# An attention and MLP kernel on one core: MLP tiles placed between the head pairs

## The chip, the cores and the metric

The kernel runs on one core of a Trainium2 chip. The metric is the device time of one execution in microseconds, as the median of several runs. A profiled execution has its own time, and its span is the time from its first to its last recorded instruction.

## The reference

```python
# q, k, v: (8, 8, 576, 64), s: (8, 8, 576); w_ch1: (512, 2048), w_ch2: (2048, 512); all float32
scores = matmul(q, k.T) / 8
cum = cumsum(maximum(s, 0))
scores = where(causal, -1e9, scores + minimum(-(cum[:, None] - cum[None, :]), 0))
scores = scores - max(scores)
attn = exp(scores);  attn = attn / (sum(attn) + 1e-9)
x = (attn @ v), heads side by side: (8, 576, 512)
u = x + real(fft(fft(x, axis=1), axis=2))
un = (u - mean(u)) / sqrt(var(u) + 1e-6)
out = u + maximum(un @ w_ch1, 0) @ w_ch2
```

## The kernel before

**Attention** goes over 32 head pairs, `i = 0..31`, four to a batch. `load` brings q and k, `high` and `low` split them into a high part and a rest (so that a product is made of two matmuls), `maxes(i)` makes 12 score matmuls (`pm`) of which DVE keeps each row's maximum, and a transpose (`pmt`) brings the maxima into a row of the q operand. `scores(i)` makes the scores again, transposed and with maximum and bias inside (`ps`, 24 matmuls), and ACT turns them into `P` with an exponential. `av(i)` multiplies by v (`pavA`, `pavB`), `recip` and `finish` divide by the row sums. In pair `i` the pieces of several pairs run together: scores of `i`, AV of `i - 1`, maxima of `i + 1`, splitting of `i + 2`.

**Fourier.** After the last pair of a batch, `folds` uses the symmetry of the transforms (DVE, ACT, POOL), and `fourier` makes two passes of matmuls (`pzs`, `pzc`, `pyc`, `pys`) and writes `u` to DRAM (`uD`). One more product for frequency 256 (`p256`) is made once for four batches. Batch `b` is folded in pair `4b + 6` and mixed in pairs `4b + 7` to `4b + 10`.

**MLP.** The 4608 tokens make nine tiles of 512. `ln_tile` reads a tile of `u`, makes means and variances with matmuls against a matrix of `1/512`, and leaves the centred values in two parts, `uch` and `ucl`, in one of two sets of buffers that tiles use in turn. For each of 16 slices `f` of the hidden width, `mlp_tile` makes twelve matmuls into a bank `h`, ACT writes `zh` (relu), DVE the rest `zl`, and twelve matmuls add to four banks `acc`. These 24 matmuls are called a block here; there are 144. The weights come as int64 words (`wP`) from which `rounded` makes float32 values in a few integer steps on DVE, ACT and POOL. `convert_w` does so for the first six slices during attention and stores them in `wD`; `load_w` takes them, or converts the other ten itself while the first MLP tile runs, and splits them into `wh` and `wl`, which then stay in SBUF.

**Order.** `weave` takes generators with a total cost each and always lets the one advance that has done the smallest share of its total. So the Python code writes instructions in an interleaved order. For TensorE this order is kept through the loop over pairs and its tail (`manual_schedule`); the other engines, and TensorE after `order.close()`, are ordered by the scheduler, which starts from it. Every engine executes its own list in order. Nearly all DMAs are issued by SP.

**PSUM** has eight banks: `ps` gives three (scores, Fourier, `h`), `psm` five (maxima, transposes, AV). For the MLP, `psm` is closed and four of its banks become `acc`.

Of the kernel before, what the change touches and what calls it, by code (L numbers as in the profile page):

```python
# [19 lines left out]
S = 576  # L20
# [7 lines left out]
NC = 6  # L28
NC1 = 4.5
N0 = 3  # L30
N1 = 8
# [10 lines left out]
def fused_kernel(ctx, tc, qkT, vA, sP, wP, tabD, tabS, corr, out):  # L42
# [7 lines left out]
    ps = ctx.enter_context(tc.tile_pool(name="ps", bufs=3, space=PSUM))  # L50
# [4 lines left out]
    wD = dram.tile([NF, 128, 1024], F32, name="wD")  # L55
# [10 lines left out]


# [4 lines left out]
    WC = 256  # L72

    def rounded(pool, f, x, bufs):

        m = pool.tile([128, WC], I32, tag="wm", name="wm", bufs=bufs)
        raw = pool.tile([128, 2 * WC], I32, tag="raw", name="raw", bufs=bufs)
        nc.sync.dma_start(out=raw, in_=wP[f, :, WC * x:WC * x + WC].bitcast(I32))
        hi = raw.rearrange("p (n w) -> p n w", w=2)[:, :, 1]
        lo = raw.bitcast(U16).rearrange("p (n w) -> p n w", w=4)[:, :, 1]  # L80
        yield 0.0
        e = pool.tile([128, WC], I32, tag="we", name="we", bufs=bufs)
# [3 lines left out]
        yield 0.4  # L86
# [3 lines left out]
        yield 0.4  # L90
        return e.bitcast(F32)

    def convert_w(pool, lo, hi, bufs):

        for f in range(lo, hi):
            for x in range(1024 // WC):
                m = yield from rounded(pool, f, x, bufs)
                nc.sync.dma_start(out=wD[f, :, WC * x:WC * x + WC], in_=m)
                yield 0.2

    def load_w(pool, f):

        wh = pool.tile([128, 1024], F32R, tag=f"wh{f}", name=f"wh{f}")
        wl = pool.tile([128, 1024], F32R, tag=f"wl{f}", name=f"wl{f}")
        W[f] = (wh, wl)
        if f < NC:
            nc.sync.dma_start(out=wl.bitcast(F32), in_=wD[f])
        n = 512 if f < NC else WC
        for x in range(1024 // n):
            xs = slice(n * x, n * x + n)  # L110
            m = wl[:, xs].bitcast(F32) if f < NC else (yield from rounded(stage, f, x, nstage))
            nc.scalar.copy(wh[:, xs], m)  # L112
            yield 0.2 * n / 512
            (nc.vector if x * n < 512 else nc.gpsimd).tensor_sub(wl[:, xs], m, wh[:, xs].bitcast(F32))  # L114
            yield 0.2 * n / 512

    def spread_sum(t, name, n):

        th = lnp.tile([128, TOK], F32R, tag="th", name="th")
        tl = lnp.tile([128, TOK], F32R, tag="tl", name="tl")  # L120
        split(th[:, :n], tl[:, :n], t[:, :n])
        m = bank(name)
# [4 lines left out]
    def ln_tile(t0, n, lag):  # L127

        u = lnp.tile([128, 4, TOK], F32, tag="u", name="u")
        (nc.sync if t0 else nc.scalar).dma_start(out=u[:, :, :n], in_=uD[:, :, t0:t0 + n].rearrange("c p t -> p c t"))  # L130
        t = lnp.tile([128, TOK], F32, tag="t", name="t")
        t2 = lnp.tile([128, TOK], F32, tag="t2", name="t2")
        nc.gpsimd.tensor_add(t[:, :n], u[:, 0, :n], u[:, 1, :n])
        nc.vector.tensor_add(t2[:, :n], u[:, 2, :n], u[:, 3, :n])
        nc.vector.tensor_add(t[:, :n], t[:, :n], t2[:, :n])
        yield lag
        pm = spread_sum(t, "mu", n)
        mlp = mlps[t0 // TOK % 2]
# [22 lines left out]

    LN, W = {}, {}

    def mlp_tile(t0, n):
        uch, ucl, mu, r = LN.pop(t0)
        last = t0 + n == NT
        if last:
# [645 lines left out]
```

## Time and profile before

| | |
|---|---|
| median of three runs | 1426.8 us (1423.96 to 1429.57) |
| profiled execution | 1426.1 us, span 1424.4 us |
| mean granted TensorE clock | 0.971 |
| busy share of the span | PE 92%, weight loads 75%, DVE 52%, POOL 39%, ACT 38% |
| DMA | 125.05 MB moved, HBM read 76.85 MB and written 23.07 MB |

PE is TensorE's matmuls, PEld its loads of weights, which overlap them. DVE, ACT and POOL are the vector, scalar and general engines. A matmul is drawn from its start to its modelled end, so two that follow each other closely overlap in the drawing, and the busy share of PE says little on how full it is. In rows of groups, `zh<-h` is what an instruction writes and reads, `x144` how often it ran, then busy time, mean ns of one, and the engine's idle time before it with what ended it.

### The profile page before, as it was taken

The numbers are of one execution on the slowest core, as the hardware profiler recorded it, in microseconds if no ns is written. First come the engines' busy times: TensorE is split into PE (matmuls) and PEld (weight loads), VectorE is DVE, ScalarE is ACT, GpSimd is POOL, SyncE is SP. The second block draws the span as 40 slices with busy tenths as digits, with TensorE's granted clock in tenths as the row PEclk, the third lists the DMA queues.
The fourth block names the chain that finished last, engine by engine and source line by source line (L and its number), as shares of the span: only waits on it lengthen the run. The fifth ranks groups of instructions, "written<-read, shape, count | busy, mean of one in ns | idle before, by whom it ended". The sixth has DMA issues, their size and how long they took to land.

```text
span 1424.4 us, 17997 instructions
## 1 busy us (share of the span) xinstructions
PE 1305.1 (92%) x6190; PEld 1068.7 (75%) x6190; DVE 745.7 (52%) x1684; ACT 539.3 (38%) x1211; POOL 561.6 (39%) x543
## 2 busy tenths in 40 slices
PE   4887979897988887997899999999999999999998
PEld 3766868686777676775688888888888888888886
DVE  6667677877777788799833233222332223322212
ACT  4775756676665656344321121211212112121110
POOL 6445465656546566565720402204022040123300
PEclk9998999999999997999899999999999999999999
DMA  8555556565655555433200000000000000000000
GB/s 214 156 159 144 163 149 180 158 168 159 159 161 144 166 149 163 162 123 121 79 8 30 31 30 15 15 30 31 30 15 15 30 30 30 15 16 0 30 0 30
DMA packets 78230, 125.05 MB, mean 88 GB/s; under 512 B 11256, under 2 KB 36249, under 8 KB 78139
## 3 DMA queue, kind: packets, MB, share of 16 engines
q1 hardware_dynamic: 75627, 119.83, 28.4%
q0 software_dynamic: 1696, 2.50, 0.9%
q10 hardware_dynamic: 816, 1.57, 0.3%
q8 instruction: 49, 0.80, 0.2%
q14 instruction: 42, 0.34, 0.1%
HBM read 76.85 MB, written 23.07 MB: 70 GB/s over the span
## 4 chain that ended last, share of the span: by engine, by line
PE 51%; DVE 7%; POOL 2%; DMA 1%; issue 1%; ACT 1%; SPq 0%; DVEq 0%; POOLq 0%; ACTq 0%
PE h L183 25%; PE acc L198 8%; PE acc L196 8%; PE acc L197 8%; POOL we L89 1%; DVE wm L88 1%; DVE we L83 1%; DVE wm L85 1%; DVE we L87 1%; DVE wl L114 1%; ACT wh L112 1%; DMA wl<-wD 0%; POOL wl L114 0%; DVE ucl L148 0%; DVE zl L188 0%
## 5 line engine op out<-in xcount | busy, mean ns | idle before, releaser
L188 DVE SCALAR_TENSOR_TENSOR zl<-h,zh 128x512 fp32r<-128x512 f32 x144 | 98.6, 686 | 405.5 <-ACT zh L187 405.4
L187 ACT ACTIVATE zh<-h 128x512 fp32r<-128x512 f32 x144 | 85.9, 596 | 530.1 <-PE h L183 530.1
L198 PE MATMUL acc<-zl,wh 128*128 128x512 f32 x576 | 227.5, 396 | 4.9 <-DVE zl L188 4.9
L196 PE MATMUL acc<-zh,wh 128*128 128x512 f32 x576 | 227.6, 395 | 1.0 <-ACT zh L187 1.0
L197 PE MATMUL acc<-zh,wl 128*128 128x512 f32 x576 | 226.8, 394 | 0.0
L523 PE MATMUL pavB<-P,va 128*128 128x320 f32 (+2 forms) x640 | 189.1, 389 | 9.5 <-ACT stage L527 8.9
L459 PE MATMUL pm<-KQ 128*128 128x256 f32 (+3 forms) x384 | 156.5, 427 | 44.4 <-DVE Mx L466 23.1
L495 ACT ACTIVATE P<-ps 128x320 f32<-128x320 f32 (+4 forms) x384 | 145.9, 393 | 110.5 <-PE ps L492 106.8
L491 PE MATMUL ps<-KQ 128*128 128x256 f32 (+2 forms) x384 | 154.1, 404 | 24.4 <-ACT P L495 14.0
L183 PE MATMUL h<-uch,wh 128*128 128x512 f32 x576 | 159.9, 398 | 8.3 <-ACT wh L112 8.3
L183 PE MATMUL h<-uch,wl 128*128 128x512 f32 x576 | 158.1, 396 | 0.8 <-DVE wl L114 0.8
L183 PE MATMUL h<-ucl,wh 128*128 128x512 f32 x576 | 156.9, 393 | 0.0
L466 DVE CUSTOM_DVE_ANT_0 trash<-pm,amask 128x128 bf16<-128x128 f32 (+3 forms) x256 | 123.5, 482 | 34.2 <-PE pm L459 16.9
L212 POOL TENSOR_TENSOR o<-o,w 128x512 f32<-128x512 f32 x32 | 41.8, 1305 | 252.3 <-issue 218.5
L183 PEld LDWEIGHTS h<-uch,wh 128*128 128x128 f32 x576 | 108.2, 190 | 35.9 <-ACT wh L112 12.1
L198 PEld LDWEIGHTS acc<-zl,wh 128*128 128x128 f32 x576 | 108.7, 189 | 32.0 <-DVE zl L188 6.9
L183 PEld LDWEIGHTS h<-uch,wl 128*128 128x128 f32 x576 | 109.2, 190 | 26.6 <-DVE wl L114 1.2
L196 PEld LDWEIGHTS acc<-zh,wh 128*128 128x128 f32 x576 | 108.6, 188 | 26.1 <-ACT zh L187 1.8
L183 PEld LDWEIGHTS h<-ucl,wh 128*128 128x128 f32 x576 | 108.9, 189 | 24.7
L197 PEld LDWEIGHTS acc<-zh,wl 128*128 128x128 f32 x576 | 108.6, 189 | 24.7
L459 PEld LDWEIGHTS pm<-KQ 128*128 128x128 f32 x384 | 78.4, 207 | 64.7 <-DVE Mx L466 30.2
L492 PE MATMUL ps<-q,k 128*128 128x256 f32 (+2 forms) x384 | 120.5, 316 | 3.1 <-POOL q L438 3.1
(140 smaller groups left out, 2066.9 us busy)
## 6 DMA issues: line engine op xcount, KB each, us to landing
qk<-in_qkT_dram SPq DMA_DIRECT2D x32, 576.0 KB
raw<-in_wP_dram SPq DMA_DIRECT2D x64, 256.0 KB
va<-in_vA_dram SPq DMA_DIRECT2D x32, 480.0 KB
q<-KQ SPq DMA_DIRECT2D x32, 288.0 KB
k<-KQ SPq DMA_DIRECT2D x32, 288.0 KB
rb<-rd SPq DMA_DIRECT2D x64, 144.0 KB
u<-uD SPq DMA_DIRECT2D x8, 1024.0 KB
out_dram<-o SPq DMA_DIRECT2D x32, 256.0 KB
```

The lines of the kernel that those rows point to most:

```text
L183: nc.tensor.matmul(h[:, :n], a[:, j * 128:(j + 1) * 128], b[:, j, :n], start=i == 0, stop=i == 11)
L187: nc.scalar.activation(zh[:, :n], h[:, :n], AF.Relu)
L188: nc.vector.scalar_tensor_tensor(out=zl[:, :n], in0=h[:, :n], scalar=0.0, in1=zh[:, :n].bitcast(F32), op0=ALU.max, op1=ALU.subtract)
L196: nc.tensor.matmul(acc[j][:, :n], a[:, cs], y[:, :n], start=g == 0, stop=False)
L197: nc.tensor.matmul(acc[j][:, :n], b[:, cs], y[:, :n], start=False, stop=False)
L198: nc.tensor.matmul(acc[j][:, :n], a[:, cs], z[:, :n], start=False, stop=g == NF - 1)
L459: nc.tensor.matmul(p[:, :n], qy[:, h, 128 * c:128 * c + 128], ky[:, h, k0:k0 + n], start=True, stop=True)
L466: nc.vector.tensor_tensor_reduce(out=trash[:nq, :n], in0=p[:nq, :n], in1=amask[:nq, m0:m0 + n], scale=1.0, scalar=first if x else NEG, op0 ...
L491: nc.tensor.matmul(p[:, :n], ky[:, h, ksl], qy[:, h, a:a + n], start=True, stop=False)
L492: nc.tensor.matmul(p[:, :n], k1[:, h, ksl], q1[:, h, a:a + n], start=False, stop=True)
L495: nc.scalar.activation(P[:, o:o + a + n - lo], p[:, lo - a:n], AF.Exp, scale=0.125)
L523: nc.tensor.matmul(p[:, a - lo:n], va[:, c, vs], P[:, o:o + w], start=c == 0, stop=c == cs[-1])
```

## The change

- From the tenth pair on (`M0 = 9`), each weave also holds four blocks of the MLP (`RATE = 4`), 2.5 in five more weaves after the last pair; what is left runs at the end. The generator `mlp()` runs through all 144 blocks in one go, with the layer norm of the next tile at `f` = 8, 10 and 12 or 15. It waits, by yielding, until the batch that the next tile needs is in `ready`.
- All sixteen slices of weights are converted in pairs 0 to 12, ten of them (`NC = 10`) in pairs 0 to 8, in pieces of 512 columns that use the buffers `uch` and `ucl`, the others in pieces of 256. They are split there, and both parts go to `wD`. Each block then fetches its weights, 0.5 MB for `h` and 0.5 MB for `acc`, into two buffers each (`fetch`). After the last pair, slices are kept as they are fetched: seven in room that attention leaves (`NA = 7`), nine more when Fourier is done.
- PSUM: `ps` and `psm` have four banks each until pair 9. From there `psm` is `acc`, and scores, maxima, transposes, AV, Fourier and `h` share the four of `ps`.
- Buffers: three `P` in place of four, two `qk` in place of three, one `rb`, one `xs`; Fourier and folds share their scratch. Until Fourier is done there is one set of `uch` and `ucl`. `u` is read from DRAM a quarter at a time, three times a tile, into three buffers `uj` that also hold the parts for the sums and the output.
- `p256` is made for each batch, with the frequency's column among 128 others; Fourier is mixed in two pairs (`4b + 7`, `4b + 8`), not four.

```diff
-NC = 6
-NC1 = 4.5
-N0 = 3
-N1 = 8
+NC = 10
+NA = 7
+M0 = 9
+RATE = 4
...
-    ps = ctx.enter_context(tc.tile_pool(name="ps", bufs=3, space=PSUM))
+    ps = ctx.enter_context(tc.tile_pool(name="ps", bufs=4, space=PSUM))
...
+    def convert(f, x, wc, words, m, e):
+        k, o = divmod(x * wc, 512)
+        nc.sync.dma_start(out=words, in_=wP[f, :, wc * x:wc * x + wc].bitcast(I32))
...
+        wh, wl = words[:, 0:wc], words[:, wc:2 * wc]
+        nc.scalar.copy(wh.bitcast(F32R), e.bitcast(F32))
+        (nc.gpsimd if k else nc.vector).tensor_sub(wl.bitcast(F32R), e.bitcast(F32), wh.bitcast(F32))
+        yield 0.3
+        nc.sync.dma_start(out=wD[f, :, k, :, o:o + wc], in_=words.bitcast(F32).rearrange("p (s n) -> p s n", s=2))
...
+    def fetch(k, s):
+        if s >= NS:
+            return
+        f = s % NF
...
+        if f not in W and rooms:
+            W[f] = x = rooms.pop(0).tile([128, 2, 2, 512], F32R, tag=f"W{f}", name=f"W{f}")
+            for h in (k, 1 - k):
+                nc.sync.dma_start(out=x[:, h].bitcast(F32), in_=wD[f, :, h])
+        if f in W:
+            uses[k, s] = W[f][:, k]
+            return
+        w = mlp0.tile([128, 2, 512], F32R, tag=f"w{k}", name=f"w{k}", bufs=2)
+        nc.sync.dma_start(out=w.bitcast(F32), in_=wD[f, :, k])
+        uses[k, s] = w
...
+    def output(x, acc, r):
+        t0, n = tiles[x]
+        for j in range(4):
+            u = uload(x, j)
+            o = mlp0.tile([128, TOK], F32, tag="uj", name="o", bufs=3)
+            nc.vector.tensor_mul(o[:, :n], r[:, :n], acc[j][:, :n])
+            nc.gpsimd.tensor_add(o[:, :n], o[:, :n], u[:, :n])
+            nc.sync.dma_start(out=out[j, :, t0:t0 + n], in_=o[:, :n])
...
+    def mlp():
...
+        for s in range(NS):
+            x, f = divmod(s, NF)
...
+            fetch(0, s + 2)
+            yield C1
+            if x + 1 < len(tiles):
+                early = len(mlps) > 1
+                if f == 8:
+                    while min(x + 1, NB - 1) not in ready:
+                        yield 1.0
+                    lnp[x + 1] = sums(x + 1)
+                if f == 10:
+                    mean(x + 1, *lnp.pop(x + 1))
+                    go = 12 if early else NF - 1
+                if f >= 11 and f == go:
+                    centre(x + 1)
...
+                yield from second(accs[y], held, [(0, j) for j in range(4)], tiles[y][1])
+                del held[0]
+            held.append((uses.pop((1, s)), zh, zl, f))
+            fetch(1, s + 1)
+            if f == 0 and x:
+                output(x - 1, accs.pop(x - 1), rs.pop(x - 1))
...
-    psm = attb_ctx.enter_context(tc.tile_pool(name="psm", bufs=5, space=PSUM))
+    psm = psm_ctx.enter_context(tc.tile_pool(name="psm", bufs=4, space=PSUM))
...
+        if i < M0 + 4:
+            share = NC / (M0 - 0.5) if i < M0 else (NF - NC) / 3.5
+            streams.append([take(weights, share), share + 0.001])
+        if i == M0 - 1:
+            streams.append([later(take(stages, 6), 7), 13])
+        if i == M0:
+            psm_ctx.close()
+            psm = None
+            accp = ctx.enter_context(pool("accp", space=PSUM))
+        if i >= M0:
+            quota = (RATE if i < NP else 2.5) * (C1 + 4 * C2)
+            streams.append([take(stages, quota), quota])
```

How the order changes at two places. TensorE, in a pair in the middle of the loop, before (`pzs` is Fourier, numbers behind a name are buffers):

```order
L523 MATMUL pavA<-P,va 128x256
L459 MATMUL pm<-KQ_121 128x256
L284 MATMUL pzs<-dsin_81,Do_2744 96x256
L284 MATMUL pzs<-dsin_82,Do_2744 96x256
L284 MATMUL pzs<-dsin_81,Do_2745 96x256
L284 MATMUL pzs<-dsin_81,Do_2744 96x256
L284 MATMUL pzs<-dsin_82,Do_2744 96x256
L284 MATMUL pzs<-dsin_81,Do_2745 96x256
L491 MATMUL ps<-KQ_120 128x256
L492 MATMUL ps<-q_2922,k_2923 128x256
L459 MATMUL pm<-KQ_121 128x256
```

and after:

```order
L247 MATMUL h<-uch,w_4769 128x512 x8
L247 MATMUL h<-ucl,w_4769 128x512 x4
L537 MATMUL pm<-KQ_118 128x512
L569 MATMUL ps<-KQ_120 128x448
L570 MATMUL ps<-q_4581,k_4582 128x448
L537 MATMUL pm<-KQ_118 128x256
L537 MATMUL pm<-KQ_118 128x320
L217 MATMUL acc_3949<-zh,w_4804 128x512
L218 MATMUL acc_3949<-zh,w_4804 128x512
L219 MATMUL acc_3949<-zl,w_4804 128x512
L537 MATMUL pm<-KQ_118 128x256
```

Twelve matmuls of `h` and the triples of `acc` now stand between maxima and scores, and `h`, `pm` and `ps` take the same four banks in turn, so that the fifth fill from an `h` on needs a bank that ACT and DVE have emptied.

DVE in a pair near the fourth, before: `we` and `wm` are the converter's, `trash` and `Mx` the maxima's.

```order
L466 ISA Mx_128 128x1
L83 TENSOR_SCALAR we<-raw 128x256
L85 TENSOR_SCALAR wm<-raw 128x256
L88 SCALAR_TENSOR_TENSOR wm<-raw,wm 128x256
L87 SCALAR_TENSOR_TENSOR we<-raw,we 128x256
L466 ISA trash,Mx_128<-pm,amask 128x256
```

and after, where `wide` holds all of the converter's parts:

```order
L89 SCALAR_TENSOR_TENSOR wide<-wide 128x512
L88 SCALAR_TENSOR_TENSOR wide<-wide 128x512
L94 TENSOR_TENSOR wide<-wide 128x512
L84 TENSOR_SCALAR wide<-wide 128x512
L86 TENSOR_SCALAR wide<-wide 128x512
L89 SCALAR_TENSOR_TENSOR wide<-wide 128x512
L88 SCALAR_TENSOR_TENSOR wide<-wide 128x512
L544 ISA trash,Mx_127<-pm,amask 128x256
```

Two pieces of the converter, twice as wide and with the split (L94), stand ahead of a read of maxima where one short piece stood.

More of the change, by code (lines that the diff above doesn't have):

```diff
@@ L224, in fused_kernel @@
     nc.vector.memset(eh.bitcast(F32), 0.0)
[L225 to L227 removed]
     rows = fft.tile([96, S], F32, name="rows")
[L229 to L230 removed]
+    x256 = rows[0:1]
     def load_tables():
@@ L567, in call @@
         fn(*args)
[L569 removed]
+    for i in range(min(2, NP)):
         load(i)
@@ L659, in ahead @@
-    def ahead():
-        while next(feed, None) is not None:
-            yield 1.0
-    op = None
-    feed = rest()
-    for x, (t0, n) in enumerate(tiles):
-        streams = [[mlp_tile(t0, n), NF]]
-        if x == 0:
-            streams.append([chain(idle(1000), mixing), FOURIER * 0.6])
-            streams.append([ahead(), 100])
-        if x + 1 < len(tiles):
-            streams.append([later(ln_tile(*tiles[x + 1], 1), 4 if x else 9), 12])
-        weave(*streams)
+            att_ctx.close()
```

426 lines of the change are left out of this document (206 added, 220 removed).

## The prediction

> **What bounds the kernel now.** I read the page first, then the windows by stage, the chain, the timeline of TensorE inside the attention loop, the waits, and the groups by shape. The windows (us, then busy us of PE, PEld, DVE, ACT and POOL, the granted clock, DMA share, GB/s) cut the run into the loop over head pairs, its tail, the first MLP tile, and the other eight:
>
> ```profile
> 25.60:545.00 519.40, 445.96 (x2490) 376.28 (x2490) 378.32 (x1073) 330.19 (x822) 292.75 (x302) 0.95 0.58 160
> 545.00:572.00 27.00, 20.81 (x102) 17.57 (x101) 23.06 (x41) 17.02 (x37) 17.46 (x14) 0.75 0.52 155
> 572.00:704.60 132.60, 113.49 (x483) 87.53 (x482) 117.44 (x247) 56.13 (x125) 79.88 (x87) 0.95 0.36 124
> 704.60:1424.40 719.80, 714.17 (x3096) 580.72 (x3094) 207.58 (x271) 125.73 (x213) 152.78 (x113) 1.00 0.06 22
> ```
>
> In the last stage TensorE is never free and every other engine is under a third busy. The chain shows its rhythm (start, length): one f step of the MLP, a block here, every 5.56 us, and one tile in 89.8 us (882.51 to 972.28).
>
> ```profile
> 882.51 5.60 PE h L183 x24
> 890.87 2.80 PE h L183 x12
> 896.43 2.80 PE h L183 x12
> ...
> 972.28 5.46 PE h L183 x24
> ```
>
> 144 blocks are 801 us, more than half of the run, and nothing in the change makes a block shorter. What can be won is TensorE's idle time elsewhere. The page's 92% for PE hides it, because the drawn length of a matmul overlaps the next one. The distance from start to start tells more. In a dense piece of the loop:
>
> ```profile
> 312.10 0.28 PE L459 MATMUL pm<-KQ 128*128 128x256 f32 x1
> 312.22 0.31 PE L491 MATMUL ps<-KQ 128*128 128x320 f32 x1
> 312.37 0.31 PE L492 MATMUL ps<-q,k 128*128 128x320 f32 x1
> 312.52 0.28 PE L459 MATMUL pm<-KQ 128*128 128x256 f32 x1
> 312.63 0.70 PE L523 MATMUL pavB<-P,va 128*128 128x320 f32 x2
> 312.93 0.80 PE L306 MATMUL pyc<-scos,zc 96*128 96x290 f32 x3
> 313.57 0.34 PE L459 MATMUL pm<-KQ 128*128 128x384 f32 x1
> 313.75 0.28 PE L491 MATMUL ps<-KQ 128*128 128x256 f32 x1
> 313.87 0.28 PE L492 MATMUL ps<-q,k 128*128 128x256 f32 x1
> 313.99 0.39 PE L459 MATMUL pm<-KQ 128*128 128x512 f32 x1
> 314.22 0.49 PE L523 MATMUL pavB<-P,va 128*128 128x192 f32 x2
> ```
>
> 256 columns take 0.12 us, 320 take 0.15, 384 take 0.18, 512 take 0.23; an AV matmul of 320 is two passes, 0.30. By these, and 0.20 for 448 columns in proportion, a pair's own work is 24 score matmuls 3.4 us, 12 for the maxima 1.8, 14 AV matmuls 3.2 and the transpose: 8.5 us. A batch's Fourier part (75 matmuls of 256 to 290 columns) is about 9.6, so 2.4 a pair. That is 10.9 us. The transposes of the maxima, one a pair, come every 16.2 us ((523.4 - 20.5)/31); the other two rows are the 10th and the 14th:
>
> ```profile
> L471 PE MATMUL pmt<-ident,Mx x32: 270/272/374, 20.5 to 523.4; 128*10 128x128 f32 x32
> 153.22 0.27 PE L471 MATMUL pmt<-ident,Mx 128*10 128x128 f32 x1
> 220.64 0.27 PE L471 MATMUL pmt<-ident,Mx 128*10 128x128 f32 x1
> ```
>
> So TensorE waits some 5.3 us in each pair. The waits that the profile can see are short ones, on maxima and exponentials that have to leave their banks:
>
> ```profile
> PE pm L459 <- DVE Mx L466: 22.4, 11, 5.5
> PE ps L491 <- ACT P L495: 14.0, 17, 2.2
> ```
>
> **The change part by part.** I add four stages, cut at the 10th and the 14th transpose. The profiled execution took 1426.1 us, span 1424.4, and the median is 1426.8, so 1.7 us lies around the span.
>
> *A, to the 10th transpose (153.2 us before).* No MLP yet. Ten of the sixteen weight blocks are converted here instead of about 1.3, each now split into high and low parts as well. The load on DVE in two windows, and, from the groups by shape, the converter's work on it (busy us, mean ns):
>
> ```profile
> 25.60:153.50 127.90, 105.54 (x546) 87.02 (x546) 87.84 (x256) 82.14 (x202) 60.64 (x65) 0.92 0.64 163
> 0.00:25.60 25.60, 10.64 (x25) 6.65 (x26) 19.26 (x54) 10.25 (x15) 18.75 (x30) 1.00 0.68 201
> ```
>
> ```profile
> L83 DVE TENSOR_SCALAR we<-raw 128x256 int32<-128x256 int32 x64 | 29.1, 457 | 1.6 <-DMA raw<-in_wP_dram 1.5
> L85 DVE TENSOR_SCALAR wm<-raw 128x256 int32<-128x256 int32 x64 | 26.0, 406 | 0.0
> L87 DVE SCALAR_TENSOR_TENSOR we<-raw,we 128x256 int32<-128x256 int32 x64 | 31.5, 495 | 0.4 <-ACT we L84 0.2
> L88 DVE SCALAR_TENSOR_TENSOR wm<-raw,wm 128x256 f32<-128x256 uint16 x64 | 31.8, 496 | 1.1
> L114 DVE TENSOR_TENSOR wl<-we,wh 128x256 fp32r<-128x256 f32 x20 | 9.7, 487 | 2.3 <-ACT wh L112 2.2
> ```
>
> The four operations are 1.85 us for 256 columns, 7.4 a block, and half of the split 1.0: 8.4. In pieces of 512 columns some of that is saved; I take 6.9. Then 10.3 x 6.9 - 1.3 x 7.4 = 61 us more. DVE was busy 87.8 + 19.3 = 107 us: 168 of work in what were 153 us. DVE becomes the bound of this stage. The least is 168; at the 0.886 that DVE reaches in the first MLP tile (117.44 of 132.60) it is 190. The converter has only two buffers and each step hops between four engines, so I stay near the upper end: 185, +32. ACT and POOL gain about 3 and 5 us a pair and stay under 0.8.
>
> *B, to the 14th transpose (67.4 us before).* The remaining six blocks of weights are converted in 256-column pieces, and the order shows 4, 4, 1 and 1 MLP blocks in these four intervals: each tile's layer norm waits for a batch that is Fourier-mixed one and a half pairs later. TensorE needs 4 x 8.5 + 10 x 5.56 + 10.8 - 4 = 96 us. For DVE:
>
> ```profile
> 153.50:220.90 67.40, 58.08 (x337) 49.49 (x337) 49.06 (x141) 43.93 (x110) 37.88 (x40) 0.95 0.58 164
> ```
>
> ```profile
> L187 ACT ACTIVATE zh<-h 128x512 fp32r<-128x512 f32 x144 | 85.9, 596 | 530.1 <-PE h L183 530.1
> L188 DVE SCALAR_TENSOR_TENSOR zl<-h,zh 128x512 fp32r<-128x512 f32 x144 | 98.6, 686 | 405.5 <-ACT zh L187 405.4
> ...
> L159 DVE RECIPROCAL r<-r 128x512 f32<-128x512 f32 x9 | 30.1, 3339 | 4.7 <-ACT r L158 4.7
> L148 DVE TENSOR_TENSOR ucl<-u,uch 128x512 fp32r<-128x512 f32 x36 | 27.4, 801 | 6.4 <-ACT uch L147 6.4
> ```
>
> 49 there now, 5.3 weight blocks x 8.4 = 45, less 4 for today's, 10 zl x 0.69 = 7, and about 13 of layer norm (eleven operations at 0.8 and one reciprocal): 110. Between TensorE's 96 and DVE's 110/0.886 = 124 I take the latter, 123: DVE is again the longer one.
>
> *C, the next 18 pairs.* 73 blocks stand in them. TensorE: 18 x 8.5 + 73 x 5.56 + 4 batches x 10.8 + 4 for means and variances = 606 us, 33.7 a pair. DVE has about 12 a pair from the loop (378/32), 2.8 of zl and 4 of layer norm, under 0.6 of it, and ACT under 0.5. What TensorE waits on top is not shown by any row, because eight banks (three and five) become four that scores, maxima, AV, Fourier and h share in one order. Nearest rows: the MLP stage, where 714.17 of 719.80 is busy, gives nothing; the loop gives 5.3 a pair with twice the banks, so up to about 8. In favour of the low end, a fill now has on average 33.7/36 = 0.94 us of other work on either side, and h leaves its bank in 0.60 + 0.69 us. Against it, maxima and scores still stand in runs, and there is a new wait: while attention lives there is only one uch/ucl set, so the next tile is centred after the last h of this one, four times an ACT copy and a DVE subtraction (0.8) behind 3 to 5 us of TensorE work, then the four output products must free acc through three "uj" buffers. I give 2 us a pair to the banks and 5 a tile to that: 3.2 a pair, 58. C is 664 (606 to 750).
>
> *D, the rest.* 61 blocks, 339 us; the last pair's attention and two Fourier batches 32; means and two extra halves of a block 9; 18 for the chain of the last batch (norm, xs, folds) and the acc hand-over of four tiles; 6 from the last matmul to the end, as now: 404 (386 to 425).
>
> Weights by DMA: 1.05 MB a block, 4.2 a pair. At the rate of the MLP stage (22 GB/s at a share of 0.06, 367 GB/s) that is 11.4 us of all sixteen engines; the loop's own 0.58 of 16.2 is 9.4 and u, out and uD about 3.5: 24 of 37 us. It is covered, and fetch(0, s+2) has more than a block of cover; if SP stood behind one load for over 8 us, TensorE would wait for w. The added p256 matmuls cost 1.2 us a batch and are counted.
>
> Sum: 185 + 123 + 664 + 404 = 1376, with 1.7 outside the span 1378 us, 3.4% less than the median.
>
> **The rivals.** *Nearly all idle time goes.* If DVE fills A to its 168, B falls to 106, C waits 12 us in all and D 386: 168 + 106 + 618 + 386 + 2 = 1280. For it speaks the MLP stage, which loses nothing with three banks; against it the runs of short fills.
>
> *Four banks make the woven stage wait more than the loop does (slower).* TensorE's order is fixed, so one late maximum stops MLP matmuls too, which had no such neighbour. For it: the waits above, up to 5.5 us at once, with five banks for maxima alone. At 7 us a pair C is 606 + 126 = 732 and the run 1446. It is slower than 1434 from (58 + 56)/18 = 6.3 us a pair on.
>
> *There is little idle time to fill (no change).* Loads of weights are busy 376.28 of 519.40 in the loop, 0.724, and 580.72 of 719.80, 0.807, where TensorE is saturated. If 0.807 is what full looks like, the loop holds 466 us of work, 131 more than my 335 (32 pairs less what runs after 545 us), of which 92 fall in pairs that get MLP; the waits there are then 1.7 a pair at most and my 58 and 18 shrink by about 45: 1378 + 92 - 45 = 1425. Against it stand the dense rows, where loads follow each other closer than their own length:
>
> ```profile
> 312.11 0.19 PEld L491 LDWEIGHTS ps<-KQ 128*128 128x128 f32 x1
> 312.23 0.19 PEld L492 LDWEIGHTS ps<-q,k 128*128 128x128 f32 x1
> 312.37 0.19 PEld L459 LDWEIGHTS pm<-KQ 128*128 128x128 f32 x1
> ```
>
> A full loop would show 1.0, not 0.807. The Trainium skill, Perfetto Trace Analysis, section Identifying the Most-Contended Engine, says that headroom on TensorE is judged by the busy share of LDWEIGHTS and not of matmuls; by that page's measure this rival is the forecast, and these rows disagree with reading it across stages with matmuls of different widths.
>
> **How the numbers follow.** Forecast (1300 to 1419): 0.60. Nearly all idle time goes: 0.14. No idle time to fill: 0.09. Banks, slower: 0.17. Half a per cent, 7 us, is about what a measurement of this kernel tells from no change, so 1419.7 to 1433.9 is "same": faster 0.74, same 0.09, slower 0.17. The range 1285 to 1450 takes the lower end of the second case and most of the slower one; its ends leave out 0.15.
>
> **What would show it.** The 10th transpose at about 185 us with DVE over 0.85 busy before it, and the 14th at about 308. Between them and the 32nd, a transpose every 37 us, with DVE below 0.65 and the granted clock at 1.0. The last stage has h again every 5.56 us. I am wrong if transposes in the woven stage come over 41 us apart, with waits of h or pm for DVE or ACT (banks) or for w (DMA), or if they come at 34.

## The result: 1567 us, 9.7% slower

The changed kernel takes 1567.3 us (median of four runs, 1557.9 to 1571.1), the kernel before 1427.3 beside it: ratio 1.097, 95% interval 1.092 to 1.103. The forecast was 1378, and its range ended at 1450. The profiled execution has a span of 1568.6 us.

The transposes of the maxima cut it into the forecast's four stages. The group, and the 10th and 14th of it in the timeline (start, length):

```profile
L549 PE MATMUL pmt<-ident,Mx x32: 270/272/415, 20.5 to 1160.3; 128*10 128x128 f32 x32
253.58 0.27 PE L549 MATMUL pmt<-ident,Mx 128*10 128x128 f32 x1
432.09 0.27 PE L549 MATMUL pmt<-ident,Mx 128*10 128x128 f32 x1
```

| stage | forecast | measured |
|---|---|---|
| A, to the 10th transpose | 185 | 253.6 |
| B, to the 14th | 123 | 178.5 |
| C, to the 32nd | 664 | 728.2 |
| D, the rest | 404 | 408.3 |

The windows (us, then busy us of PE, PEld, DVE, ACT, POOL, clock, DMA share, GB/s) about these stages, with C in two pieces, since its first two pairs are not like the others:

```profile
25.00:250.00 225.00, 149.03 (x608) 119.52 (x608) 139.82 (x330) 103.41 (x237) 102.06 (x94) 0.78 0.61 175
250.00:430.00 180.00, 128.36 (x583) 101.28 (x582) 93.15 (x229) 73.83 (x167) 62.02 (x67) 0.85 0.61 182
430.00:545.00 115.00, 78.24 (x341) 61.36 (x340) 56.10 (x130) 39.95 (x91) 40.27 (x38) 0.85 0.62 197
545.00:1160.00 615.00, 592.39 (x2937) 494.37 (x2936) 287.62 (x657) 244.40 (x538) 181.42 (x180) 0.99 0.66 200
1160.00:1568.60 408.60, 389.26 (x1760) 322.22 (x1758) 113.79 (x170) 80.82 (x153) 49.18 (x47) 0.97 0.38 126
```

In the first, DVE is busy 0.62 of the time (139.82 of 225), not 0.886: it is not the bound there, and no engine is. The clock is 0.78. Who waits: SP, whose list also holds every load of q, k and v and the row of maxima (`mt`). Its waits in 25 to 250 us, the longest groups (us in total, times, longest):

```profile
SPq L96 <- POOL wide L94: 45.4, 10, 8.2
SPq L96 <- DVE wide L94: 26.1, 5, 7.8
SPq L552 <- ACT P L573: 18.3, 4, 8.6
SPq L96 <- DVE Mx L544: 16.9, 4, 8.9
SPq L96 <- DMA wide<-in_wP_dram: 10.5, 5, 3.8
```

L96 is the converter's write-back. With two more rows, of 8.5 and 2.9, SP stands there 110 us of 225. In its timeline the rows of cumulative sums for a pair's keys (`cumD`) are issued until 71.85, then nothing for 11 us, and the row sums (`sums`) come behind the write:

```profile
70.82 1.03 SPq L494 DMA_DIRECT2D KQ<-cumD  x1
83.05 0.33 SPq L96 DMA_DIRECT2D wD<-wide  x1
83.91 0.80 SPq L610 DMA_DIRECT2D sums<-stage  x1
```

TensorE's longest waits in 25 to 253:

```profile
PE ps L569 <- DMA KQ<-mt: 23.4, 7, 7.3
PE pm L537 <- DVE Mx L544: 19.8, 15, 3.3
```

From 253 to 546, in B and the first two pairs of C, three waits stand out. The first is for the sums of the first MLP tile, the others are for weights (`w`):

```profile
PE mu L149 <- ACT th L74: 26.4, 1, 26.4
PE h L247 <- DMA w<-wD: 19.8, 1, 19.8
PE acc L217 <- DMA w<-wD: 6.1, 2, 6.0
```

The forecast named such a wait for `w` as a sign of being wrong. In SP's list nothing fetches weights for 21 us; between the two fetches stand the transfers of a pair and those of the converter's last, narrow pieces, of which these are the last two:

```profile
484.20 0.37 SPq L130 DMA_DIRECT2D w<-wD  x1
502.93 0.38 SPq L96 DMA_DIRECT2D wD<-narrow  x1
505.15 0.34 SPq L80 DMA_DIRECT2D narrow<-in_wP_dram  x1
505.55 0.43 SPq L130 DMA_DIRECT2D w<-wD  x1
```

In the woven stage proper, 545 to 1160:

```profile
PE h L247 <- ACT uch L185: 12.0, 4, 3.7
PE pm L537 <- DVE Mx L544: 2.6, 7, 0.9
PE ps L569 <- DVE yp L394: 2.4, 4, 0.6
PE ps L569 <- ACT P L573: 2.2, 5, 1.1
```

Apart from the 12.0 for `uch`, the waits of 0.8 us and more are some 10 us in 615, so four banks cost little that the profile shows. The rival on banks was wrong, although the time came out slower.

### The profile page after: what moved, and what is told of

Its sections match the earlier page's. It is cut to its first block, busy times and chain, and to the rows that moved or that the text cites. A ratio compares the mean times of both kernels' runs of the same rounds, so it can differ in the third digit from the quotient of the medians.

```text
span 1568.6 us, 18552 instructions
## 1 busy us (share of the span) xinstructions
PE 1347.2 (86%) x6244; PEld 1104.4 (70%) x6244; DVE 709.0 (45%) x1562; ACT 550.0 (35%) x1195; POOL 453.7 (29%) x456
## 4 chain that ended last, share of the span: by engine, by line
PE 51%; DMA 6%; issue 4%; DVE 4%; ACT 1%; POOL 1%; SPq 0%; DVEq 0%; POOLq 0%
PE h L247 19%; PE acc L217 6%; PE acc L218 6%; PE acc L219 6%; PE pavB L601 5%; DMA uj<-uD 5%; PE ps L569 2%; PE ps L570 2%; PE pm L537 1%; PE pavA L601 1%; PE pyc L380 1%; PE pys L389 1%; PE pzc L369 1%; PE pzs L361 1%; DVE ucl L186 1%
## 5 line engine op out<-in xcount | busy, mean ns | idle before, releaser
L247 PE MATMUL h<-uch,w 128*128 128x512 f32 x792 | 208.8, 405 | 47.7 <-ACT uch L185 26.3
L247 PEld LDWEIGHTS h<-uch,w 128*128 128x128 f32 x792 | 149.5, 194 | 83.8 <-ACT uch L185 30.7
L601 PEld LDWEIGHTS pavB<-P,va 128*128 128x128 f32 x640 | 128.0, 209 | 55.2 <-issue 10.8
L217 PE MATMUL acc<-zh,w 128*128 128x512 f32 x384 | 156.7, 408 | 6.7 <-DMA w<-wD 6.1
L218 PE MATMUL acc<-zh,w 128*128 128x512 f32 x384 | 152.2, 396 | 0.0
L219 PE MATMUL acc<-zl,w 128*128 128x512 f32 x384 | 152.1, 396 | 0.0
L569 PEld LDWEIGHTS ps<-KQ 128*128 128x128 f32 x384 | 79.3, 206 | 67.6 <-DMA KQ<-mt 25.0
L516 POOL TENSOR_TENSOR q<-qk,q 64x576 fp32r<-64x576 f32 x64 | 95.1, 1504 | 70.4 <-DMA q<-KQ 64.8
L247 PE MATMUL h<-ucl,w 128*128 128x512 f32 x396 | 111.1, 403 | 0.8 <-DVE ucl L186 0.8
L247 PE MATMUL h<-uch,W 128*128 128x512 f32 x360 | 91.8, 398 | 0.0
L247 PEld LDWEIGHTS h<-ucl,w 128*128 128x128 f32 x396 | 77.7, 196 | 18.3 <-DVE ucl L186 1.2
L570 PEld LDWEIGHTS ps<-q,k 128*128 128x128 f32 x384 | 79.3, 206 | 8.6
```

Of the source, the lines that this page charges most:

```text
L217: nc.tensor.matmul(acc[j][:, :n], b[:, 0, cs], y[:, :n], start=g == 0, stop=False)
L218: nc.tensor.matmul(acc[j][:, :n], b[:, 1, cs], y[:, :n], start=False, stop=False)
L219: nc.tensor.matmul(acc[j][:, :n], b[:, 0, cs], z[:, :n], start=False, stop=g == NF - 1)
L247: nc.tensor.matmul(h[:, :n], w[:, a, j * 128:(j + 1) * 128], b[:, j, :n], start=i == 0, stop=i == 11)
L516: nc.gpsimd.tensor_sub(q1[64:128, h], qk[0:64, h], q1[0:64, h].bitcast(F32))
L569: nc.tensor.matmul(p[:, :n], ky[:, h, ksl], qy[:, h, a:a + n], start=True, stop=False)
```

## The experiments

"Without conversion" is e3. Times are of the profiled execution, one run each beside a run of the kernel before, unless an interval is given. DVE's, ACT's, POOL's and SP's lists are ordered by a scheduler; only TensorE's is written by hand, and from the loop over pairs on it is that of the changed kernel in e1 to e10 and e16 (in e6 without the AV matmuls left out). The kernel before, run beside these, has spans of 1419.9 to 1431.4 us, so totals that differ by under some 10 us are not told apart.

| run | span | 10th | to 14th | to 32nd | rest |
|---|---|---|---|---|---|
| before | 1424.4 | 153.2 | 67.4 | 302.8 | 901.0 |
| after | 1568.6 | 253.6 | 178.5 | 728.2 | 408.3 |
| e1 no arithmetic | 1449.6 | 186.8 | 158.0 | 699.6 | 405.3 |
| e2 no transfers | 1495.8 | 235.3 | 151.7 | 699.0 | 409.8 |
| e3 no conversion | 1424.5 | 178.5 | 136.7 | 699.8 | 409.5 |
| e4 write late | 1539.5 | 225.8 | 178.9 | 730.2 | 404.5 |
| e5 no hops | 1492.6 | 246.3 | 142.1 | 698.8 | 405.5 |
| e6 AV thinned | 1415.7 | 167.4 | 134.7 | 707.1 | 406.4 |
| e7 skewed | 1540.8 | 224.2 | 161.4 | 746.4 | 408.7 |
| e8 all before | 1518.8 | 274.7 | 142.8 | 698.0 | 403.3 |
| e9 DVE's part only | 1450.5 | 208.8 | 136.0 | 696.3 | 409.4 |
| e10 ACT's and POOL's only | 1453.4 | 207.6 | 137.8 | 697.8 | 410.2 |
| e11 before, no conversion | 1402.8 | 151.9 | 69.4 | 302.2 | 879.4 |
| e12 gentle | 1533.6 | 214.1 | 98.0 | 663.7 | 557.9 |
| e13 before, small buffers | 1449.7 | 157.3 | 70.2 | 321.2 | 900.9 |
| e14 before, dense | 1520.5 | 224.3 | 105.3 | 299.3 | 891.6 |
| e15 before, both | 1530.7 | 223.6 | 105.8 | 306.9 | 894.4 |
| e16 no conversion, three qk | 1412.0 | 170.2 | 135.6 | 698.0 | 408.2 |
| e17 before, ten blocks at 0.28 a pair | 1489.3 | 172.7 | 76.7 | 343.2 | 896.7 |
| e18 before, dense, write late | 1492.8 | 227.0 | 67.6 | 303.9 | 894.3 |

**The conversion in parts.** In `convert`, e1 leaves out the arithmetic, from its first line to its last, and sends a constant at the write:

```diff
-        nc.vector.tensor_scalar(e, hi, 0x7FF00000, None, op0=ALU.bitwise_and)
...
-        (nc.gpsimd if k else nc.vector).tensor_sub(wl.bitcast(F32R), e.bitcast(F32), wh.bitcast(F32))
```

e2 leaves out the transfers, and e3 both:

```diff
-        nc.sync.dma_start(out=words, in_=wP[f, :, wc * x:wc * x + wc].bitcast(I32))
+        nc.gpsimd.memset(words, 0)
...
-        nc.sync.dma_start(out=wD[f, :, k, :, o:o + wc], in_=words.bitcast(F32).rearrange("p (s n) -> p s n", s=2))
...
-        nc.sync.dma_start(out=w.bitcast(F32), in_=wD[f, :, k])
+        nc.sync.dma_start(out=w.bitcast(F32), in_=wD[0, :, k])
```

> Left out: the converter's arithmetic and split; both transfers stay, and the write-back sends a constant tile, so SP has nothing to wait for at it (the weights are then constants, and the order of TensorE is that of the changed kernel). The changed kernel has its 10th transpose of the maxima at 253.6 us, 178.5 to the 14th, 728 to the 32nd, 408 after it. Theory 1 (SP stands in its list at the write-back until the split is done, and what is queued behind it is late): the stand is gone; 10th transpose at 150 to 170, 100 to 120 to the 14th, total 1390 to 1425. Theory 2 (the bytes of the conversion crowd the DMA engines): nothing changes, 1540 to 1570. Theory 3 (DVE, ACT and POOL are too loaded with the arithmetic): as theory 1. Theory 4 (fewer buffers for P, qk, rb and maxima): 1540 to 1570.

> Left out: both transfers of the converter (the raw words are set to zero by POOL, some 1 us a piece more for POOL; all blocks of the MLP fetch the same first weight block of DRAM, which is written once); the arithmetic stays. Theory 1 (SP stands at the write-back): SP has no write-back, so 10th transpose at 165 to 190, total 1390 to 1430. Theory 2 (bytes): the same. Theory 3 (arithmetic load): still 240 to 255 at the 10th transpose, 1530 to 1570. Theory 4 (fewer buffers): 1530 to 1570.

> Left out: the whole conversion, transfers and arithmetic (all blocks fetch the same first weight block, written once); the order of TensorE stays. What is left over the woven forecast is the cost of the smaller buffers. Theories 1 to 3: 10th transpose at 140 to 155, 95 to 115 to the 14th, total 1370 to 1400. Theory 4 (fewer buffers): 10th transpose still over 220, total over 1520.

Without conversion the span is 144.1 us shorter. With the transfers alone it is 25.1 over that, with the arithmetic alone 71.3, together 144.1: 48 us exist only when both are there, which is when SP has arithmetic to wait for. So theory 1 can hold for a third at most, theory 3, which is the forecast's own in a wider form, holds for half, and the bytes of theory 2 for at most the 25. Theory 4 (smaller buffers), which expected e3 above 1520, fails. None of the three totals lies in a range that was expected of theory 1 or 3. In e2 and e5 the scheduler moved 256-column pieces ahead (DVE had run 62 and 85 of their 108 operations when the tenth set of maxima was read, and e5's 246.3 lies above both of its ranges), so I compare these two by their totals. And e3 shows what no theory had: without any conversion the woven kernel only reaches the time of the kernel before.

**Moving the write-back.** In e4, `back` issues the write of the piece before and `ahead` a read two pieces on:

```diff
+            steps = convert(n // 2, n % 2, 512, words[n], me[:, 0:512], me[:, 512:1024])
+            yield next(steps) / 2
+            back(n - 1)
+            yield next(steps) / 2
+            ahead(n + 2)
```

> All work is done. Only the place and the buffers of the converter's transfers change: the raw words go round four buffers (those of w0 and w1, idle until the MLP starts), each read is issued more than one piece ahead and each write-back a third of a piece after the next has begun; the 256-column pieces keep one buffer, with write and read some steps apart. Theory 1 (SP stands at the write-back): most of the loss goes, 10th transpose at 175 to 195, 120 to 145 to the 14th, total 1400 to 1450. Theory 2 (bytes) and theory 3 (arithmetic load) and theory 4 (fewer buffers): the same bytes, work and buffers, 1540 to 1570.

SP's waits at the write-back, now L82, in 25 to 250 us:

```profile
SPq L82 <- POOL words L98: 10.9, 4, 4.0
SPq L82 <- DVE narrow L98: 10.3, 2, 7.1
```

With the smaller rows they are 39 us instead of 110, and the 10th transpose comes 28 us earlier. That is a part of the loss, not most of it: 47 us over the run without conversion stay, and the total is in the range of the other theories. Nor is SP's standing a loss by itself. Its other waits grew in e4: at the sending of the maxima 18.3 us (L552 above) became 41.0. And in e3, which has no write-back, SP's nine longest groups of waits are 87 us of the 153 from 25 to 178:

```profile
SPq L577 <- ACT P L598: 41.0, 6, 8.4
```

```profile
SPq L511 <- PE ps L562: 27.1, 7, 6.9
SPq L602 <- ACT stage L599: 25.2, 7, 8.7
```

e7 lets piece n - 1 and piece n of e4 take their steps in turn:

```diff
+            if n:
+                next(steps[n - 1])
...
+                next(steps[n])
```

> As the run with late write-backs (all work done), and two pieces are in work at once, half a piece apart, so that each step's input from another engine was issued half a piece earlier; same operations, bytes and buffers. That run has the 10th transpose at 225.8 us, 178.9 to the 14th. Theory 3b (hops between engines that run in order): 190 to 208 at the 10th, total 1505 to 1525. Theory 3a (load): 220 to 230, total 1535 to 1545. In both the 14th comes 170 to 185 later, since the 256-column pieces stay as they are.

Nothing: 224.2 against 225.8. Theory 3b, that steps wait for another engine's step, fails here.

e8 is e4 with

```diff
-NC = 10
+NC = 16
```

> As the run with late write-backs, and all sixteen blocks of weights are converted ahead of the MLP in 512-column pieces, so that no 256-column piece with its one buffer stands in SP's list among fetches of weights and rows. If those pieces are what the 14th transpose and the first two woven pairs lose (42 and 28 us against the run without conversion): 140 to 155 us from the 10th to the 14th, about 700 to the 32nd; the 10th pays six more blocks at 4.7 us each, 245 to 260; total 1490 to 1515. If the loss there has another cause: 170 to 185, 720 to 730, total 1550 to 1575.

Stages B and C fall to 142.8 and 698.0, as without conversion, 68 us less than in e4. So the 256-column pieces beside the first woven pairs were their loss, and e8 has no wait for `w` there. The six blocks cost 49 us in A instead, more than the 28 expected.

**Load or hops, and whose load.**

In e5 `c` is one constant tile, and `d`, `a` and `p` belong to DVE, ACT and POOL:

```diff
-        nc.scalar.copy(wh.bitcast(F32R), e.bitcast(F32))
+        nc.scalar.copy(a.bitcast(F32R), c.bitcast(F32))
```

> As the run without transfers, but each of the converter's operations on the first ten blocks reads one constant tile and writes a tile of its own engine, so that DVE, ACT and POOL do the same operations in the same places and none of them waits for another (the weights are left out, and so are POOL's settings to zero of that run, 0.95 us for each of 20 pieces). That run has its 10th transpose at 235.3 us, the one without any conversion at 178.5. Theory 3a (the sheer load on DVE, ACT and POOL): 220 to 235. Theory 3b (each piece hops DVE, ACT, DVE, POOL, ACT, DVE or POOL, every engine runs its list in order, and so maxima and exponentials stand behind a step that waits for another engine): 180 to 200.

The total is that of the run without transfers (1492.6, 1495.8), so hops between engines cost nothing that shows here either. e9 keeps only the `nc.vector` lines of this for all blocks, e10 only the `nc.scalar` and `nc.gpsimd` lines.

> As the run without hops, for all sixteen blocks in 512-column pieces, and only DVE's operations of the converter are left in (no transfers, no ACT and no POOL operation; the weights are left out). The run without any conversion took 1426 us, the one without hops 1494. If DVE's load is what the arithmetic costs: 1475 to 1500. If ACT or POOL is: 1425 to 1445.

> The counterpart: only ACT's and POOL's operations of the converter are left in. If DVE's load is what the arithmetic costs: 1425 to 1445. If POOL's or ACT's is: 1465 to 1500.

Both lie between their ranges: DVE's operations alone cost 26 us, ACT's and POOL's alone 29. In the window 25 to 205 us of e9 and of e10:

```profile
25.00:205.00 180.00, 134.31 (x613) 108.22 (x613) 162.44 (x387) 83.20 (x203) 69.49 (x70) 0.90 0.48 120
```

```profile
25.00:205.00 180.00, 126.39 (x613) 104.63 (x614) 80.97 (x244) 116.94 (x263) 113.57 (x118) 0.87 0.50 122
```

In e9 DVE is 0.90 busy and all sixteen blocks' share is done at 208.8 us; in e10 ACT and POOL are at 0.65 and 0.63, full nowhere, and the stage is as long. The clock explains neither (0.90 and 0.87; 0.89 in e3), and in e10 DVE's own operations are no slower than in e3 (80.97 us for 244, 80.14 for 245). A pair passes through all lists in turn (copies, maxima, the row of maxima through SP, exponentials, masks, sums), so work that is put into any list makes the pair longer before that engine is full. That this is the mechanism is a reading that fits e10's row, while in e9 DVE alone comes near its limit; no run singles it out.

**The price of an AV matmul.** e6 is e3 with

```diff
+                cs = [cs[0], cs[-1]]
```

> As the run without any conversion, but three of the five AV matmuls of the second group are left out for every head, two of 320 columns and one of 192, that is 2 x 3 in a pair. The forecast priced a 320 matmul at 0.30 us from one spacing; matmuls of AV that stand next to each other are 0.27 apart for each of their two records, 0.54 together, and 0.325 for 192. If 0.54 is the price (so that the loop before had 2.1 us a pair less idle time than forecast), 18 pairs from the 14th to the 32nd transpose lose 18 x 2 x (2 x 0.538 + 0.325) = 50 us: 650 after 699.8. If 0.30 is, 28 us: 672. If the woven stage is not bound by TensorE, less than 15.

Between the 16th and the 31st transpose, twelve of the pairs fell from 38.3 us on average to 35.7, 2.6 less, where 0.54 gave 2.8 and 0.30 gave 1.6. The sum missed all the same. C did not get shorter (707.1 us), which was expected of a stage that TensorE does not bound: every fourth pair, the one with the change of tile, rose from 38 to 47. In the windows of this stage (399 to 1015) the waits of h for uch went from 13.0 to 19.7 us, those of acc for the output's products from 0.4 to 15.5, and the clock from 0.99 to 0.96. Late loads show as one reason. In e3 three of the next tile's four quarters of `u` are asked for before the last h of the old tile (825.99), in e6 one is (last h at 812.68), at this change and at the other three alike. SP's list, which the scheduler made anew, has them further back:

```profile
799.89 0.41 SPq L128 DMA_DIRECT2D uj<-uD  x1
802.58 0.58 SPq L128 DMA_DIRECT2D uj<-uD  x1
812.21 0.57 SPq L128 DMA_DIRECT2D uj<-uD  x1
827.21 0.32 SPq L128 DMA_DIRECT2D uj<-uD  x1
```

```profile
796.35 0.41 SPq L128 DMA_DIRECT2D uj<-uD  x1
813.49 1.37 SPq L128 DMA_DIRECT2D uj<-uD  x3
820.41 0.69 DVE L176 TENSOR_TENSOR uj<-uj,mu 128x512 f32<-128x512 f32 x1 [1.62 <-DMA uj<-uD]
```

Whether this is all of the rise is not shown. So the price rests on the twelve pairs, whose pace followed TensorE's work. TensorE at this change in e6 (start, length; in brackets the idle time before and who ended it):

```profile
817.53 0.40 PE L239 MATMUL h<-uch,w 128*128 128x512 f32 x1
821.81 0.80 PE L239 MATMUL h<-uch,w 128*128 128x512 f32 x1 [3.88 <-ACT uch L177]
823.04 0.80 PE L239 MATMUL h<-uch,w 128*128 128x512 f32 x1 [0.44 <-ACT uch L177]
824.25 2.50 PE L239 MATMUL h<-uch,w 128*128 128x512 f32 x5 [0.41 <-ACT uch L177]
826.54 1.47 PE L239 MATMUL h<-ucl,w 128*128 128x512 f32 x4
```

**Is it the order, the buffers or the pace?**

e11 is the kernel before, with its converter gone and in `load_w`

```diff
+        nc.sync.dma_start(out=wh.bitcast(F32), in_=wD[0])
+        nc.sync.dma_start(out=wl.bitcast(F32), in_=wD[0])
```

> The kernel before, with its conversion left out: no raw words, no arithmetic, no split; every weight block is fetched from the same block of DRAM, written once. This is the counterpart of the run of the changed kernel without conversion (1426 us). If the kernel before also pays for its conversion (its first MLP tile has 132.6 us where the later ones have 89.8, and the loop some more): 1355 to 1390, and then weaving in itself costs time. If its conversion is hidden: 1410 to 1425, and the woven order by itself is worth nothing either way.

1402.8: the kernel before pays 21.6 us for its conversion, all behind the loop (32nd transpose at 523.4 in both). That is between the two expectations. Against this run, weaving by itself costs 21.7 us (e3). Taking 5.56 us for each block: A +26.6, B 136.7 - 69.4 - 10 x 5.56 = +11.7, C 699.8 - 302.2 - 73 x 5.56 = -8.3, the rest 409.5 - 879.4 + 83 x 5.56 = -8.4. So weaving wins 17 us behind the 14th transpose and loses 38 ahead of it.

e12 is e8 with

```diff
-M0 = 9
+M0 = 17
```

> As the run with all blocks converted ahead, with the MLP from the 18th pair on instead of the 10th, so that the conversion goes at 0.97 blocks a pair instead of 1.88. All work is done. That run took 1520.5 us. If the loss is conversion that is too dense for DVE, and weaving a pair earns nothing (3.1 us of waits in a woven pair against 3.2 of idle time in one that is not): 1450 to 1485. If each woven pair earns the idle time that the forecast gave it, eight woven pairs less cost 8 x 2 to 3 us more than the gentler pace gives back: 1515 to 1550.

The total is where the second case put it, but for another reason: at half the pace, the eight pairs from the 10th to the 18th transpose take 23.6 us on average, in the kernel before 16.9. That is 6.7 us for 0.97 blocks. The first nine blocks were cheaper, 4.0 each (214.1 against the 178.5 of e3; DVE had then done 81 of its 144 operations). Over all sixteen it is about 5.4 a block, with e11's 17.3 us a pair in place of e3's woven pairs, against 6.0 in e8. The price hardly falls with the pace.

e13 is the kernel before with the changed one's buffers:

```diff
-            P = attb.tile([128, PW], F32, tag="P", name="P", bufs=4)
+            P = attb.tile([128, PW], F32, tag="P", name="P", bufs=3)
...
-        qk = atop.tile([128, 2, S], F32, tag="qk", name="qk", bufs=3)
+        qk = atop.tile([128, 2, S], F32, tag="qk", name="qk", bufs=2)
```

> The kernel before with the buffers of the changed one: three instead of four for P, two instead of three for qk (with the load three pairs ahead issued after a pair's order instead of ahead of it), one instead of two for rb, four banks for maxima and AV instead of five and four instead of three for the rest. Its conversion and MLP are its own. Before: 10th transpose at 153.2 us, 32nd at 523.4, total 1424.4. If the buffers are what the changed kernel loses to the 10th transpose without any conversion (178.5 against 151.9): 165 to 178 at the 10th, 560 to 620 at the 32nd. If not: 150 to 157, and 515 to 535.

+4 us to the 10th, +25 over the loop: buffers are a small part of A.

e14 is the kernel before with

```diff
-NC = 6
+NC = 10
...
-        share = NC1 * 4.0 / (NP - 2) if i < NP - 2 else (1.0, 4.0)[i - NP]
+        share = 40 / 8.5 if i < 9 else 0.0
```

> The kernel before with its own buffers and its own converter (256-column pieces, no split, one set of buffers), but ten blocks converted in the first nine pairs of the loop, 1.18 a pair instead of 0.15, as the changed kernel paces it. If dense conversion costs by itself, whatever the buffers (5 to 7 us a block in the changed kernel): 10th transpose at 195 to 225 us instead of 153.2. If it costs because the changed kernel has less slack: 155 to 170.

As expected of the pace, or rather of the quantity: +71 to the 10th. SP stands at the write-back there too (25 to 250 us):

```profile
SPq L98 <- POOL we L89: 88.6, 32, 9.9
```

e15 has the edits of e13 and e14.

> Both edits on the kernel before: the smaller buffers and the dense conversion. If the two costs only add: the sum of the two runs' differences at the 10th transpose. If the small buffers are what makes conversion expensive: 15 us more than the sum or above.

223.6: at the 10th not even the sum. The small buffers do not make conversion dear.

e16 is e3 with

```diff
-        qk = atop.tile([128, 2, S], F32, tag="qk", name="qk", bufs=2)
+        qk = atop.tile([128, 2, S], F32, tag="qk", name="qk", bufs=3)
```

and `load(i + 3)` ahead of a pair's streams.

> The changed kernel without any conversion, with the third qk buffer of the kernel before and its load of three pairs ahead back at the head of each pair (the room is that of the converter). The run without conversion has its 10th transpose at 178.5 us. If the late load of q and k is what the first pairs lose: 155 to 168, total 1400 to 1415. If another buffer, or the order: 174 to 182, total 1420 to 1430.

170.2, 8.3 less than e3, between the two expectations; the total, 1412.0, is 12.5 less, and leaves 9.2 over e11. Of the 26.6 us, 9.4 are 71 Fourier matmuls at 0.133 that the new order places before the 10th transpose instead of behind it; with 8.3 for q and k some 9 stay open.

e17 is the kernel before with

```diff
-NC = 6
+NC = 10
-NC1 = 4.5
+NC1 = 8.5
```

> The kernel before with ten blocks converted in the loop instead of six, at 0.28 a pair instead of 0.15 (it loses nothing in the loop at 0.15; at 1.18 a pair it loses some 9 us a block). All work is done, and four blocks less are converted beside the first MLP tile, where conversion costs it 22 us in all. If a block costs the same at any pace: 40 us more in the loop, 1440 to 1460. If a slow pace hides in the pairs' idle time: the loop stays within 5 us, the MLP's first tile saves up to 8, 1415 to 1428.

1490.5 us, ratio 1.042 (1.039 to 1.044). Neither case: the loop grew by 69 us for four blocks, 17 each, even at 0.28 a pair. In 25 to 500 us SP stood at the write-back:

```profile
SPq L98 <- POOL we L89: 79.8, 23, 9.2
```

In the kernel before this wait is 8.6 us, 3 times. The loop's first blocks are free there, the next are not, and the 71 us more of SP's stand go with the 69 us of the loop. That the one makes the other is not shown: SP's other waits shrank, so that its seven longest groups are 177 us against 163.

e18 is e14 with two sets of raw words and results, and in `convert_w`

```diff
+            yield 0.3
+            back()
...
+            ahead(n + 1)
```

> The kernel before at the dense pace (ten blocks in nine pairs), with two sets of raw words and results, each read issued half a piece ahead and each write-back half a piece after its arithmetic. Dense without that: 10th transpose at 224.3 us, SP standing 89 us at the write-back; no dense conversion: 153.2. If SP's stand at the write-back is what delays the pairs: 165 to 190 at the 10th. If the added work on DVE, ACT and POOL and the bytes do: 205 to 225.

227.0, and SP still stands 76 us of 200 at the write: the scheduler left the write near the arithmetic. The loop ends 30 us earlier than e14's (598.5 against 628.9 at the 32nd transpose), all of it after the 10th. So the run does not separate the stand from the work; it stays open how much of the kernel before's cost is SP's.

No run is faster than the kernel before with all the work done.

## Why the prediction was wrong, step by step

- **Price of AV, 3.2 us a pair.** This is the step that failed first. It read 0.30 us for a matmul of 320 columns from the distance to the next row, 312.63 to 312.93. But that next row, three `pyc` matmuls of 290 columns, then took 0.64 us where three take 0.40 (0.134 each, the median in the trace): the start of the next matmul is drawn early, and the time turns up behind it. Where ten records of AV stand together, five matmuls of 1216 columns in all, they show their price:

```profile
234.31 2.38 PE L601 MATMUL pavB<-P,va 128*128 128x320 f32 x10
236.49 0.47 PE L537 MATMUL pm<-KQ 128*128 128x512 f32 x1
```

  2.18 us for 1216 columns; two records for 320 are 0.269 apart, 0.54 together. The Trainium skill, FP8 and Floating Point Precision, section TensorE Precision Notes, says that true FP32 takes four passes through the array; the trace agrees, 0.54 against 0.146 for a score matmul of 320. A pair's 3200 columns are 5.4 us. A pair then needs 13.1 and not 10.9 us of 16.2, and idle are 3.1, not 5.3. e6 agrees: 2.6 us a pair, where this price gives 2.8.
- **C, 58 us of waits.** With AV at 5.4 the 606 become 646, and e3's 699.8 leaves 54 us, 3.0 a pair, where the term was 58. Its split was not right: 2 us a pair went to the banks, and the waits shown on them are some 10 us in sixteen pairs. What makes up the rest is open, so that the sum came out is partly luck. But 3.0 us of waits in a woven pair against 3.1 of idle time in a plain one is no gain. The other 28 us of the changed kernel are its first two pairs (51.9 and 63.0 us), late behind the 256-column pieces (e8); 26 us of them are TensorE's waits for `w`.
- **A, "DVE becomes the bound of this stage", 0.886 busy.** The work on DVE was sized right: 67.8 us for ten blocks, forecast 6.9 each. That it alone sets the stage was wrong: 0.62 busy, and ACT's and POOL's part costs as much as DVE's (e9, e10). B was taken from DVE too (124 worked out, 123 entered), and there DVE is 0.52 busy; its longest wait is the 26.4 us for the first tile's sums, 8.3 in e3. A is 75 us over the run without conversion, B 42, where the forecast gave 32 to A for conversion.
- **What was priced at nothing.** SP was named only for late weights in the woven stage, and these came (19.8 us at once). Nothing was said of its stand at the write-back in A: 110 us, and with 71 less of it the 10th transpose came 28 us earlier (e4). Nor was anything said of what the new order and buffers cost in A without conversion: 26.6 us (e3 against e11).
- **The clock at 1.0** holds in the woven pairs (0.99), not in A (0.78), so that the work between the waits is slower too.
- **D** (404, measured 408.3), the uch change (5 us a tile, measured 3.0) and the banks as no cause of a slower run were about right. In the last stage the chain has h every 5.44 us, as forecast or a little better:

```profile
1312.67 2.72 PE h L247 x12
1318.11 2.72 PE h L247 x12
```

- **The rival "There is little idle time to fill"** had the better view of the loop. That the kernel without conversion takes 1426.4 us, where the rival said 1425, is luck: its figure holds 32 us of conversion in A. The rows that I set against it are loads for score matmuls of 256 and 320 columns, 0.12 to 0.14 apart; they say nothing of AV's, which stand 0.27 apart. Its rule, LDWEIGHTS as the measure, gave 131 us of work more than my count; the AV correction alone gives 32 x 2.2 = 70.

Together: 1376 forecast, +48.5 from e3 (-6.5 in A, 13.7 in B, 35.8 in C, 5.5 in D; AV's price is 40 in C), +144 for conversion: 1568.6. The forecast's A already held 32 us for conversion, and e3 has none, so in A the cost of order and buffers hides behind it.

## What to carry to other kernels

Price a matmul from a run of its own kind, start to start: across a change of kind the trace can move its time into the next row. Before weaving work into idle time, compare the idle time per step with the waits that the woven step will have; equal numbers mean no gain, whatever the busy shares say. And when work is added to a pipeline that passes through every engine and the DMA issuer in turn, no engine has to be full for it to cost: measure a small dose first, and look at what is queued behind each transfer that waits for an engine.

## What was not expected of the hardware

After a wait of 3.88 us TensorE ran at half speed: the h matmuls of e6 above follow each other at 0.46 us (five in 2.29), where they are 0.227 apart in a dense piece. In e3 a wait of 3.03 us was followed by the same (five in 2.30), and the granted clock is 0.50 from 681.25 to 684.67. But after 3.37 us in the same run the next five stay fast (1.26 us), and the slow ones come behind them:

```profile
681.45 2.50 PE L239 MATMUL h<-uch,w 128*128 128x512 f32 x5 [3.03 <-ACT uch L177]
683.75 0.63 PE L239 MATMUL h<-ucl,w 128*128 128x512 f32 x1
```

```profile
681.25:684.67 3.42, 3.23 (x8) 2.55 (x9) 0.69 (x1) 0.77 (x2) 3.08 (x2) 0.50 0.21 70
```

```profile
1127.13 1.46 PE L239 MATMUL h<-uch,w 128*128 128x512 f32 x5 [3.37 <-ACT uch L177]
1128.39 1.90 PE L239 MATMUL h<-ucl,w 128*128 128x512 f32 x4
```

The Trainium skill, TensorE: Matmul & The Clock Gate, section Part 1: The HAM clock gate, says that the clock falls to a half after an idle window of about 3.4 us. The wait of 3.88 us agrees; the one of 3.03 is under that figure, and after the one of 3.37 the fall came late, so in these traces the length of a wait alone does not settle it. Where the clock falls, the one wait at a change of tile costs more than its own length.
